# Releasing K's weights at the start: a gate of two elements in place of a gate behind a large write

## The chip, the cores and the metric

The kernel runs on one core of one Trainium2 chip. The metric is the device time of one execution in microseconds (us), the median over several executions. Each execution also gives the span of the core (first to last instruction, some 1.7 us shorter than the time) and the mean granted clock of TensorE. A profile is one execution; its times count from the start of the span.

## The reference, cut to what matters

```python
x  = A_x                                   # 2048 x 576
xn = layernorm(x)
q, k, v = split_heads(xn @ wqkv)           # 32 heads of 18
pq, pk  = phi(q), phi(k)                   # phi(t) = t + 1 or exp(t), plus 1e-6
o   = linear_attention(pq, pk, v)
out = x + o @ wo + (gelu(xn @ w_gate) * (xn @ w_up)) @ w_down
```

The first 14 us of the kernel: the first tiles of x (128 rows each) are loaded, normalised and transposed, K's 576 x 576 weights are loaded, and the first products xn @ K are made.

## The kernel before: the parts that the argument touches

The loads. SP issues x; ScalarE issues K's weights (`which == 1`) once, at the start; Q's weights and the next tiles of x are let go later, by another two-element write.

```python
def load_x(n0, cnt):
    nc.sync.dma_start(x_sb[:, n0:n0 + cnt, :], x_view[:, n0:n0 + cnt, :])

def load_w(which, on=nc.sync):
    c = slice(which * D, (which + 1) * D)
    on.dma_start(wqkv_sb[:, 0:4, c], A_wqkv[0:512, c].rearrange("(kt p) c -> p kt c", p=P))
    on.dma_start(wqkv_sb[0:HP, 4, c], A_wqkv[512:576, c])
    ...
nc.scalar.preload_act_table_set("natural_log_exp_and_others")
load_x(0, 1)
load_x(1, 1)
load_x(2, 2)

nc.vector.memset(wqkv_sb[HP:P, 4, :], 0.0)          # L119: zero padding, 64 x 1728
nc.vector.memset(wqkv_sb[0:1, 0, D:D + 2], 0.0)     # L120: two elements inside K's target
load_w(1, nc.scalar)                                # so K's load waits for L120
...
spin(NWARM)                                         # 38 filler matmuls: TensorE busy from 1.43 to 5.22 us
```

The second write is a gate. It touches two elements that K's load overwrites, so the load has to wait for it; and because VectorE works in order, it also waits for the large write ahead of it.

## Time and profile before

The time before was 523.56 us (three executions, 523.36 to 523.85). What matters of its trace:

| event | us |
|---|---|
| K's first load issued by ScalarE / landed | 1.95 / 7.37 |
| x tile 1 issued / landed | 1.26 / 3.51 |
| x tiles 2 and 3 issued / landed | 1.73 / 5.64 |
| first transpose of tile 0 on TensorE | 5.48 |
| first K product | 7.41 |
| second half of tile 2's K product (from here on TensorE is the bound) | 12.04 |

The list of loads in the first 20 us, with size and time from issue to landing in the last column:

```profile
wqkv_sb<-in_A_wqkv_dram ACTq DMA_DIRECT2D x1, 576.0 KB, 5.4
...
x_sb<-in_A_x_dram SPq DMA_DIRECT2D x2, 144.0 KB, 2.3
x_sb<-in_A_x_dram SPq DMA_DIRECT2D x1, 288.0 KB, 3.9
```

Line by line: K; x tiles 0 and 1; x tiles 2 and 3.

### The profile page before, as it was taken

How to read it: one execution, taken by the hardware profiler on the slowest of the kernel's cores; microseconds unless marked ns; L12 is line 12 of the kernel's file. 1: busy time of each engine (PE TensorE's matmuls, PEld its weight loads, DVE VectorE, ACT ScalarE, POOL GpSimd, SP SyncE). 2: the span in 40 equal slices, each digit the busy share in tenths (PEclk: the TensorE clock that was granted, in tenths of full speed). 3: DMA queues.
4: the chain of work that ended last, by engine and by line, in shares of the span. 5: the costliest groups of instructions: out<-in, count | busy, mean ns of one | idle time of the engine just before them, and what ended most of it. 6: DMA issues, size and time to landing. Idle time of an engine off the chain costs nothing.

```text
span 521.7 us, 10641 instructions
## 1 busy us (share of the span) xinstructions
PE 516.1 (99%) x4498; PEld 313.5 (60%) x4498; DVE 250.9 (48%) x436; ACT 143.1 (27%) x293; POOL 35.2 (7%) x55
## 2 busy tenths in 40 slices
PE   7999999999999999999999999999999999999997
PEld 6777755555587754444577744444777544445775
DVE  7996565876358323433388133333584233433101
ACT  6898442332320013323200032232000123322000
POOL 2021000211001100000012000000011000000000
PEclk9999999999999999999999999999999999999999
DMA  8334609899500045555300155555100355440000
GB/s 279 62 64 118 154 25 264 254 269 266 157 12 13 13 124 155 144 156 160 93 13 13 41 166 145 155 156 155 29 23 13 103 161 158 140 134 2 13 11 24
DMA packets 106282, 57.89 MB, mean 111 GB/s; under 512 B 13370, under 2 KB 105722, under 8 KB 106234
## 3 DMA queue, kind: packets, MB, share of 16 engines
q1 hardware_dynamic: 105626, 56.55, 38.8%
q8 instruction: 35, 0.57, 0.5%
q10 hardware_dynamic: 608, 0.66, 0.4%
q14 instruction: 13, 0.11, 0.1%
HBM read 52.86 MB, written 2.36 MB: 106 GB/s over the span
## 4 chain that ended last, share of the span: by engine, by line
PE 97%; DMA 1%; ACT 1%; DVE 0%; issue 0%
PE ps_all L313 55%; PE ps_all L677 27%; PE ps_all L289 4%; PE ps_all L682 4%; PE ps_all L245 3%; PE ps_all L342 3%; DMA wqkv_sb<-in_A_wqkv_dram 1%; PE ps_all L451 1%; PE ps_all L433 0%; PE ps_all L659 0%; ACT xnT L234 0%; ACT L114 0%; ACT phi_e L265 0%; ACT phi_e L269 0%; DVE hT L273 0%; DVE res L685 0%
## 5 line engine op out<-in xcount | busy, mean ns | idle before, releaser
L313 PE MATMUL ps_all<-xnT,wg 64*128 64x512 bf16 x1152 | 272.6, 376 | 0.0
L313 PE MATMUL ps_all<-xnT,wu 64*128 64x512 bf16 x1152 | 271.8, 376 | 0.0
L648 DVE TENSOR_TENSOR hT<-ps_all,gl 128x512 bf16<-128x512 f32 x144 | 99.5, 691 | 161.9 <-ACT gl L647 161.2
L647 ACT ACTIVATE gl<-ps_all 128x512 f32<-128x512 f32 x144 | 86.1, 598 | 314.3 <-PE ps_all L313 297.4
L313 PEld LDWEIGHTS <-wu 64*128 64x128 bf16 x1152 | 108.3, 94 | 66.3
L313 PEld LDWEIGHTS <-wg 64*128 64x128 bf16 x1152 | 108.3, 94 | 66.1
L677 PE MATMUL ps_all<-wd_sb,hT 128*128 128x288 bf16 x1152 | 147.0, 286 | 0.0
L677 PEld LDWEIGHTS <-hT 128*128 128x128 bf16 x1152 | 112.3, 98 | 30.6 <-issue 1.3
L475 DVE RECIPROCAL den_sb<-den_sb 126x128 f32<-126x128 f32 (+1 forms) x80 | 68.3, 911 | 0.5
L685 DVE TENSOR_TENSOR res<-ps_all,x_sb 128x288 bf16<-128x288 f32 x32 | 14.7, 458 | 88.0 <-PE ps_all L682 88.0
L313 PE MATMUL ps_all<-xnT,wr 64*128 64x512 bf16 x288 | 55.1, 376 | 0.0
L478 POOL TENSOR_TENSOR pqT<-pqT,den_sb 126x512 bf16<-126x512 bf16 (+3 forms) x25 | 24.2, 966 | 317.3 <-DVE den_sb L475 279.4
L682 PE MATMUL ps_all<-m_sb,pqT 126*128 126x288 bf16 (+1 forms) x160 | 24.9, 285 | 0.0
L313 PEld LDWEIGHTS <-wr 64*128 64x128 bf16 x288 | 14.4, 94 | 16.9 <-issue 0.7
L245 PE MATMUL ps_all<-wqkv_sb,xnT 128*128 128x288 bf16 x160 | 22.5, 286 | 0.9 <-DMA wqkv_sb<-in_A_wqkv_dram 0.8
L289 PE MATMUL ps_all<-hT,xn 128*128 128x288 bf16 (+4 forms) x176 | 22.4, 275 | 0.0
L289 PEld LDWEIGHTS <-xn 128*128 128x128 bf16 (+1 forms) x176 | 17.5, 102 | 4.1
L245 PEld LDWEIGHTS <-xnT 128*128 128x128 bf16 x160 | 15.4, 98 | 6.9 <-issue 1.4
L682 PEld LDWEIGHTS <-pqT 126*128 126x128 bf16 (+1 forms) x160 | 15.5, 97 | 4.1
L342 PE MATMUL ps_all<-xnT,wqkv_sb 128*126 128x512 bf16 (+1 forms) x70 | 17.4, 378 | 0.0
L273 DVE SCALAR_TENSOR_TENSOR hT<-ps_all,phi_e 128x288 bf16<-128x288 f32 x32 | 13.2, 450 | 4.6 <-ACT phi_e L269 4.0
L265 ACT ACTIVATE phi_e<-ps_all 128x288 f32<-128x288 f32 x32 | 12.9, 410 | 3.6 <-PE ps_all L245 2.1
(68 smaller groups left out, 173.8 us busy)
## 6 DMA issues: line engine op xcount, KB each, us to landing
wg<-in_B_w_gate_dram SPq DMA_DIRECT2D x72, 256.0 KB, 2.9
wu<-in_B_w_up_dram SPq DMA_DIRECT2D x72, 256.0 KB, 3.5
wd_sb<-in_B_w_down_dram SPq DMA_DIRECT2D x12, 432.0 KB, 4.6
wr<-in_B_w_gate_dram SPq DMA_DIRECT2D x72, 32.0 KB, 2.7
wr<-in_B_w_up_dram SPq DMA_DIRECT2D x72, 32.0 KB, 3.1
out_dram<-res SPq DMA_DIRECT2D x15, 144.0 KB, 1.8
x_sb<-in_A_x_dram SPq DMA_DIRECT2D x3, 576.0 KB, 7.1
wqkv_sb<-in_A_wqkv_dram SPq DMA_DIRECT2D x2, 576.0 KB, 4.7
```

The costliest lines, as they stand in the source:

```text
L245: nc.tensor.matmul(ps_all[:, k_bank(n, hf), :HALF], lhsT=xnT[:, kt, n * P:(n + 1) * P], rhs=wqkv_sb[:, kt, D + hf * HALF:D + (hf + 1) * HALF],
L273: nc.vector.scalar_tensor_tensor(out=out_, in0=ps, scalar=0.0, in1=e, op0=ALU.max, op1=ALU.add)
L289: nc.tensor.matmul(ps_all[:m, b, col:col + w], lhsT=xn[:, n, j0:j0 + m], rhs=pk[:, n, d0:d0 + w], start=(n == 0 and col == 0), stop=(n == ...
L313: return nc.tensor.matmul(self.outs[i], lhsT=self.lhs(i, rows, kt), rhs=self.rhs(i, rows, kt), start=start, stop=stop, skip_group_check=True,)
L342: nc.tensor.matmul(ps, lhsT=wqkv_sb[:, kt, q0:q0 + rows], rhs=xnT[:, kt, sc * SC:(sc + 1) * SC], start=(kt == 0), stop=(kt == KT - 1),)
L475: nc.vector.reciprocal(out=d[:, h:h + P], in_=d[:, h:h + P])
L478: nc.gpsimd.tensor_tensor(out=pqT[:rows, c, cols], in0=pqT[:rows, c, cols], in1=d, op=ALU.mult)
L647: nc.scalar.activation(out=gl[:], in_=ps_all[:, b[0], :], func=ACT.Gelu_apprx_tanh)
L648: nc.vector.tensor_tensor(out=hT[:, GUB * k + i, :], in0=ps_all[:, b[1], :], in1=gl[:], op=ALU.mult)
L677: nc.tensor.matmul(acc, lhsT=hT[:, f, j * P:(j + 1) * P], rhs=wd_sb[:, f, hs], start=(f == 0), stop=False,)
L682: nc.tensor.matmul(acc, lhsT=pqT[:rows, c, ts_], rhs=m_sb[:rows, c, hs], start=False, stop=(c == NCH - 1),)
L685: nc.vector.tensor_tensor(out=res[:, hs], in0=acc, in1=x_sb[:, n, hs], op=ALU.add)
```

## The change

The intent is to let K's weights go as soon as the program starts, behind the two-element write alone, because TensorE waits 0.8 us for them. It is one moved line:

```diff
-    nc.vector.memset(wqkv_sb[HP:P, 4, :], 0.0)
     nc.vector.memset(wqkv_sb[0:1, 0, D:D + 2], 0.0)
     load_w(1, nc.scalar)
+    nc.vector.memset(wqkv_sb[HP:P, 4, :], 0.0)
```

## The prediction

> **What bounds the kernel now.** I read the whole page first. TensorE is busy 516.1 of 521.7 us, so nothing that leaves TensorE's path as it is can move the time, and what can be won is TensorE's idle time. The view of TensorE's waits names all of it that is worth naming:
>
> ```profile
> PE ps_all L133 <- POOL ident masks.py:199: 1.4, 1, 1.4
> PE ps_all L245 <- DMA wqkv_sb<-in_A_wqkv_dram: 0.8, 1, 0.8
> PE ps_all L231 <- DVE xn L216: 0.3, 1, 0.3
> ```
>
> The reader is to see that in the whole run only one wait of TensorE belongs to the weights this change touches: one wait, 0.8 us. Then the table of windows says where it lies and that nothing after it is loose:
>
> ```profile
> 0.00:7.41 7.41, 4.86 (x52) 4.40 (x52) 5.59 (x21) 3.25 (x8) 2.99 (x16) 1.00 0.76 227
> 7.41:12.04 4.63, 4.49 (x42) 3.39 (x42) 3.34 (x11) 3.76 (x11) 0.59 (x3) 1.00 1.04 339
> 12.04:66.00 53.96, 53.96 (x415) 40.87 (x416) 41.11 (x115) 42.17 (x113) 7.44 (x12) 1.00 0.45 103
> 66.00:515.00 449.00, 449.00 (x3965) 262.07 (x3962) 200.43 (x291) 93.92 (x161) 24.15 (x25) 1.00 0.38 109
> ```
>
> Second column: the length; third: TensorE busy. From 12.04 to 515 us TensorE is busy all the time, so a start that is earlier by some tenths should reach the end whole. Third, the chain of waits over the first 16 us:
>
> ```profile
> 0.80 1.15 ACT L114
> 1.95 5.42 DMA wqkv_sb<-in_A_wqkv_dram
> 7.37 0.04 issue
> 7.41 0.79 PE ps_all L245 x5
> 8.20 0.02 issue
> 8.22 0.41 ACT phi_e L265
> ```
>
> K's weights leave at 1.95, land at 7.37, and the first K product starts 0.04 us later. The chain puts the table load ahead of the transfer, but that is only the instruction before it on ScalarE. The timeline shows what really held it:
>
> ```profile
> 0.80 1.28 ACT L114 ACT_TABLE_LOAD   x1 [0.80 <-PEq L725]
> 1.05 0.78 DVE L119 MEMSET wqkv_sb<- 64x864 uint32 x1 [1.05 <-PEq L725]
> 1.86 0.06 DVE L120 MEMSET wqkv_sb<- 1x1 uint32 x1
> 1.95 0.44 ACTq L109 DMA_DIRECT2D wqkv_sb<-in_A_wqkv_dram  x1
> ```
>
> The table load runs until 2.08, the transfer is issued at 1.95: it does not wait for the load. It comes 0.03 us after the end of the two-element write (1.86 + 0.06 = 1.92), and that write stands behind the large one on VectorE.
>
> **What the Trainium skill says.** (1) "DMA: Bandwidth & Descriptors", section "Anatomy of one DMA": DMA engines do not wait on semaphores; a wait is made on the issuing sequencer, before dispatch. The trace agrees: 1.92 to 1.95. (2) Same page, "Issuing engines are not separate DMA queues": "DMAs initiated by the scalar, sync or gpsimd engine will ultimately run on the same 16 DMA engines and interleave with each other". That is the main caution: an earlier K shares with x. The trace agrees that the engines are full: x's queue q1 and K's queue q10 together keep about 98% of the 16 engines from 2.0 to 5.6 us. (3) Same page, "Queues, rings and completion order": each DMA engine goes round between its queues packet by packet, so K will not wait until x is done once its descriptors are there. In the window 3.8 to 5.6 both queues do move (lines below). (4) "VectorE: DVE Perf Modes", section "Zero memsets can be issued as uint32": a memset takes a cycle per element. The trace has 64x864 at 778 ns, 0.90 ns per element along a row, and 59 ns for one element.
>
> **The change part by part.** It moves one line; it removes and adds none. The built programs differ only in the order of these two writes on VectorE; TensorE, ScalarE, GpSimd and SP keep their instructions, and the transfer now waits for the first VectorE signal instead of the second. The large write touches other partitions (64 to 127 of the fifth slab) than the transfers, so it gets no wait on them.
> - VectorE: the same two writes, 0.78 + 0.06 us, in the other order. Its next real work is the first x tile's statistics at 3.14, with 0.48 us idle before. Cost: 0.
> - The issue: the small write starts at 1.05, ends at 1.11, plus 0.03 gives 1.14. K's first transfer leaves 1.95 - 1.14 = 0.81 us earlier, the second (72 KB) 1.61 instead of 2.42.
> - The first packet: before, q10 moves nothing until 3.8, though K left at 1.95:
>
> ```profile
> q1 hardware_dynamic: 350, 0.46, 98.4%
> ...
> q10 hardware_dynamic: 426, 0.49, 81.7%
> q1 hardware_dynamic: 64, 0.11, 17.5%
> ...
> q1 hardware_dynamic: 93, 0.43, 79.0%
> q10 hardware_dynamic: 182, 0.18, 30.0%
> ```
>
> (Three windows: 2.0 to 3.8, 3.8 to 5.6 and 5.6 to 7.4 us; packets, MB, share of the engines.) If the 1.9 us from issue to first packet are its own, K's packets start at about 3.1. V's weights, the same shape, later show 1.25 us from issue (47.17) to first packet (48.4) on an idle queue; with that K would start at 2.4. I take 2.4 to 3.1.
> - The landing: the engines are full from 2.0 us on, so bytes are not made, only reordered. The first four tiles of x (0.59 MB) and K (0.66 MB) are 1.25 MB. But from 5.6 on K's last packets share with the next x load, of 4608-byte packets, and with 0.81 us more in front K has fewer packets left by then. Landing moves from 7.37 by less than 0.81: I take 0.4 to 0.8, so 6.6 to 7.0.
> - TensorE: the K product also needs the first tile's transposes, copied by VectorE at 6.65 to 6.89, and TensorE's filler ends at 6.62. So the start cannot come forward by more than 0.79 us.
> - The price: x tiles 2 and 3 leave at about 1.73 and land 3.9 us later, at 5.63; VectorE wants them at 5.67. There is no slack. If K pushes them to 5.9 or 6.0, the statistics there start 0.3 later, and with them, in VectorE's order, the copy for the first K product (to 6.95 to 7.19) and tile 1's normalisation. The last two of its five matmuls then start at 7.2 instead of about 7.75: about 0.5 of the 0.79 stays, and behind tile 1's transposes 0.3 to 0.4.
> - Passing on: from 8.22 to 11.5 the chain runs on ScalarE, nearly full, so an earlier first relu moves it whole; at 12.04 TensorE takes over. Later inputs have slack: x tile 4 lands at about 9.0 for 10.35, Q's weights at about 11.8 for 13.48.
>
> Sum: 0.79 at most, less 0.3 to 0.5 of delayed x: about 0.4 us. 523.56 - 0.36 = 523.2.
>
> **The rivals.** (a) Nothing lost: x keeps its times, K lands by 6.7, 0.75 us won, 522.8. For it: x's packets of 3.0 to 3.8 are alone in their queue and the bytes per us are low there (255 GB/s over the window against 332 after), so K may fill unused time. Against it: the engines count as 98% busy. (b) K takes the place of x: issued at 1.14 it is now ahead of x tile 1 (about 1.26) and tiles 2 and 3 (1.73), not behind them. If descriptors are made in order of issue, for 512 rows of K against 128 of a tile, x lands up to 1 us later, VectorE falls behind, and the wait of TensorE moves from the DMA to the copy: 0 won, or 0.3 lost, 523.6 to 523.9. For it: q10's silence until 3.8, as if K had stood in line behind x. (c) The transfer is hidden anyway: against it stands the direct release at 7.37 to 7.41. I give the main line 50%, (a) 20%, (b) 30%.
>
> **Range and chances.** Every rival lies within 0.8 us, 0.15%, of 523.56, and three runs before spread over 0.5 us. So faster or slower by over 2% (10.5 us) would need an altogether different state of the chip. The range is 522.5 to 523.9: the full win with some spread, to rival (b) with some.
>
> **What would show it.** K's issue on ScalarE's queue at about 1.14 proves the release; a first q10 packet at 2.4 to 3.1 the start; tiles 2 and 3 landing over 4.1 us after issue the price; the first L245 at 6.8 to 7.2, with its DMA wait under 0.5 us, the gain. TensorE's start of the K product, halves 0 and 1, must then be early by a like amount at 12.04. If x's statistics wait on a DMA for over 0.5 us, (b) holds. The prediction is wrong if the issue does not move (a wait on ScalarE that I do not see) or if x is starved by more than 1 us.

## More of the kernel before

The order in which each engine's instructions are written is set by a table of numbers. They sort the program text; they are no times of the chip.

```python
STEPS = [
    (ln_stats, [3.15, 4.09, 5.57, ...]),             # VectorE, tile 0, 1, 2, ...
    (ln_rstd,  [4.27, 5.21, 6.69, ...]),             # ScalarE
    (ln_norm,  [x_, 6.78, 8.06, ...]),               # VectorE; tile 0 at 5.03 and 5.41
    ...
]
todo += [(4.0, lambda n: nc.vector.memset(x_sb[0:1, n, 0:2], 0.0), 4)]
todo += [(4.01, lambda n: load_x(n, 4), n) for n in (4,)]
todo += [(4.02, lambda n: load_w(0), 0)] + [(4.03, lambda n: load_x(n, 4), n) for n in (8, 12)]
```

So VectorE takes the statistics of tiles 0 and 1, then tile 0's normalisation, then the statistics of tiles 2 and 3 and on.

## The result, and the profile after

The changed kernel took 525.40 us (median of four, 524.75 to 525.66), the one before 523.68 in the same rounds. The ratio is 1.0032, with a 95% interval of 1.0014 to 1.0049. Ratios here are the mean time of one kernel's fast executions over that of the other's in the same rounds, so they are not quite the ratio of the medians. By its interval it is slower, by about 1.7 us, where 0.4 us of gain had been predicted.

K did come early. The chain of waits of the changed kernel's first 30 us no longer has it:

```profile
1.26 4.57 DMA x_sb<-in_A_x_dram
5.83 0.02 issue
5.85 0.83 DVE stats L207 x2
6.68 0.02 issue
6.71 0.21 DVE mv L208
6.91 0.49 DVE xn L216 x2
```

In K's place stands x tile 1: issued at 1.26 as before, landed at 5.83 in place of 3.51. The list of loads says the same:

```profile
wqkv_sb<-in_A_wqkv_dram ACTq DMA_DIRECT2D x1, 576.0 KB, 4.6
...
x_sb<-in_A_x_dram SPq DMA_DIRECT2D x2, 144.0 KB, 3.6
x_sb<-in_A_x_dram SPq DMA_DIRECT2D x1, 288.0 KB, 5.0
```

The 3.6 is the median of two unlike loads (2.6 for tile 0, 4.6 for tile 1): a median of a group hides that one member went wrong. K, issued at 0.95, landed at 5.55. What the queues moved shows how. These are the window from 3.2 to 4.0 us after, then the same window before (packets, MB, share of the engines; q1 is SP's queue and carries x, q10 is ScalarE's and carries K):

```profile
q10 hardware_dynamic: 267, 0.31, 106.5%
```

```profile
q1 hardware_dynamic: 80, 0.17, 76.0%
q10 hardware_dynamic: 11, 0.01, 5.6%
```

After, not one packet of x moves in these 0.8 us, though tile 1 had been issued 1.9 us before the window begins. This is not sharing packet by packet; tile 1 stands behind K.

VectorE's timeline shows what the late tile holds up:

```profile
0.86 0.06 DVE L119 MEMSET wqkv_sb<- 1x1 uint32 x1 [0.86 <-PEq L725]
...
5.85 0.82 DVE L207 BATCH_NORM_STATS2 stats<-x_sb 128x6 f32<-128x288 bf16 x2 [1.31 <-DMA x_sb<-in_A_x_dram]
6.71 0.21 DVE L208 BATCH_NORM_AGGREGATE mv<-stats 128x2 f32<-128x12 f32 x1
6.83 0.57 DVE L216 TENSOR_SCALAR xn<-x_sb,mv,rstd 128x384 bf16<-128x384 bf16 x2
```

The bracket is idle time and what ended it. Tile 0 is on the core at 3.45, but its normalisation (6.83; 5.10 before) stands in VectorE's order behind tile 1's statistics. TensorE's wait for K, 0.8 us, is gone, and another has come:

```profile
PE ps_all L231 <- DVE xn L216: 2.0, 1, 2.0
```

That is tile 0's transpose, waiting for the normalised tile. And then the clock falls. The windows view for 8.0 to 11.4 us, before and after, where the first column after the window is its length, the next TensorE busy with its number of matmuls, and the third number from the end is the granted clock:

```profile
8.00:11.40 3.40, 3.32 (x33) 2.49 (x31) 2.27 (x7) 3.15 (x10) 0.48 (x2) 1.00 1.06 326
```

```profile
8.00:11.40 3.40, 3.40 (x23) 2.52 (x22) 2.08 (x9) 2.07 (x7) 0.47 (x2) 0.50 1.07 363
```

TensorE is "busy" all the time in both, but at half clock it did 23 matmuls in place of 33. The page would not show this by its busy shares: a throttled engine looks fuller. In numbers at TensorE: first transpose +1.73 us, first K product +0.92 (it had been 0.8 late for K before), second half of tile 2's K product +1.82. Every later point keeps this; the gate and up projections begin at 67.51 in place of 65.71.

### The profile page after: what moved, and what is told of

Its sections match the earlier page's. It is cut to its first block, busy times and chain, and to the rows that moved or that the text cites. A ratio compares the mean times of both kernels' runs of the same rounds, so it can differ in the third digit from the quotient of the medians.

```text
span 523.5 us, 10641 instructions
## 1 busy us (share of the span) xinstructions
PE 517.1 (99%) x4498; PEld 314.5 (60%) x4498; DVE 250.9 (48%) x436; ACT 143.2 (27%) x293; POOL 35.2 (7%) x55
## 4 chain that ended last, share of the span: by engine, by line
PE 98%; DMA 1%; DVE 0%; SPq 0%; issue 0%; POOL 0%; POOLq 0%
PE ps_all L313 55%; PE ps_all L677 27%; PE ps_all L245 4%; PE ps_all L289 4%; PE ps_all L682 4%; PE ps_all L342 3%; DMA x_sb<-in_A_x_dram 1%; PE ps_all L451 1%; PE ps_all L433 0%; PE ps_all L659 0%; PE ps_all L231 0%; DVE stats L207 0%; PE ps_all L133 0%; DVE xn L216 0%; DVE res L685 0%; SPq L93 0%
## 5 line engine op out<-in xcount | busy, mean ns | idle before, releaser
L245 PE MATMUL ps_all<-wqkv_sb,xnT 128*128 128x288 bf16 x160 | 23.6, 296 | 0.0
L207 DVE BATCH_NORM_STATS2 stats<-x_sb 128x6 f32<-128x288 bf16 x32 | 13.0, 448 | 2.0 <-DMA x_sb<-in_A_x_dram 2.0
```

Of the source, the lines that this page charges most:

```text
L245: nc.tensor.matmul(ps_all[:, k_bank(n, hf), :HALF], lhsT=xnT[:, kt, n * P:(n + 1) * P], rhs=wqkv_sb[:, kt, D + hf * HALF:D + (hf + 1) * HALF],
```

## The experiments

Twelve runs. The theory: **loads are handed out in one line, in about the order of their issue, whichever queue they are on**; K now stands ahead of x tiles 1 to 3, tile 1 comes 2.3 us late, and TensorE's idle gap costs it the clock on top. Rivals: the two queues share packet by packet and only K's bytes matter; VectorE's in-order work is the real loss; the clock is the whole loss. The table collects what the sections below use; "tile 2" is the start of the second half of tile 2's K product (12.04 before).

| run | K issued / landed | x tile 1 landed | x tiles 2, 3 landed | first K product | tile 2 | time, ratio [95%] |
|---|---|---|---|---|---|---|
| before | 1.95 / 7.37 | 3.51 | 5.64 | 7.41 | 12.04 | 523.6 |
| after | 0.95 / 5.55 | 5.83 | 6.73 | 8.33 | 13.86 | 525.40, 1.0032 [1.0014, 1.0049] |
| a_again | 0.95 / 5.73 | 6.00 | 6.92 | 8.36 | 13.17 | 526.05, 1.0038 [1.0026, 1.0050] |
| e1_warm | 0.95 / 5.37 | 5.68 | 6.65 | 8.04 | 12.85 | 525.13, 1.0027 [1.0015, 1.0039] |
| e2_tile0_first | 0.95 / 5.50 | 5.91 | 6.85 | 6.83 | 13.29 | 524.77, 1.0020 [1.0007, 1.0033] |
| e3_between | 1.50 / 8.14 | 3.63 | 7.13 | 8.18 | 12.86 | 524.91, 1.0025 [1.0009, 1.0041] |
| e4_behind | 1.77 / 7.27 | 3.63 | 5.49 | 7.31 | 11.94 | 523.54, 0.9995 [0.9980, 1.0009] |
| e5_slabs | 0.95 / 6.93 | 4.21 | 6.53 | 6.76 | 12.26 | 524.35, 1.0008 [0.9990, 1.0026] |
| e6_one_queue | 1.26 / 5.65 | 6.25 | 7.00 | 9.00 | 14.46 | 525.85, one look |
| e7_next_x_later | 1.95 / 6.91 | 3.48 | 4.72 | 6.95 | 11.76 | 523.42, 0.9993 [0.9978, 1.0007] |
| e8_second | 1.07 / 5.86 | 5.06 | 6.86 | 7.42 | 12.58 | 524.78, 1.0014 [0.9999, 1.0028] |
| e9_behind_later | 1.77 / 6.90 | 3.50 | 5.40 | 6.94 | 11.58 | 523.27, 0.9986 [0.9974, 0.9999] |
| e10_second_order | 1.07 / 6.27 | 5.83 | 7.09 | 8.63 | 14.22 | 524.97, 1.0019 [1.0005, 1.0032] |
| e9_again | 1.77 / 7.01 | 3.63 | 5.42 | 7.05 | 11.68 | 523.15, 0.9986 [0.9970, 1.0002] |

(K landed means its 512-row load; in e5_slabs, the last slab of it.)

Two cautions for the table. First, the trace records the arrival of each of these loads in 16 parts, and "landed" is the last of the 16. Where most parts are in time and one or two are late, the text below says so. Second, the mean granted clock counts only what the clock record holds. A mean of 1.000 does not prove a full clock: in e6 the record begins at 10.73 us and in e10 there is none, both are listed with 1.000, and in both TensorE's matmuls near 9 us start 0.24 us apart in place of 0.12. So the counts of executions with a fallen clock below are counts of falls that the record shows, and may be too low.

### a_again: the changed kernel once more

No edit.

> The changed kernel once more, beside the others. Both theories: 525.0 to 525.7 us, x tile 1 landing near 5.8 us. It also shows whether the halved clock of TensorE (8.0 to 11.4 us in the first trace) comes back in another execution.

The six executions fall in two groups. Two, of 524.5 and 524.6 us, have a granted clock of 1.000; four, of 525.95 to 526.39, have 0.996 or 0.997. The profiled one is of the first group, and in its window TensorE does 34 matmuls at full clock:

```profile
8.00:11.40 3.40, 3.33 (x34) 2.43 (x35) 2.91 (x10) 2.86 (x10) 0.47 (x2) 1.00 1.07 368
```

Its x tile 1 is as late (6.00), yet tile 2's product is at 13.17, not 13.86. So by these two traces the late tile alone costs about 1.1 us of TensorE's time, and the half clock, where it strikes, another 0.7. The two sets of the changed kernel together: five executions at full clock with a mean span of 523.28, five with the fall with 524.28. The kernel before, beside all the experiments, had the fall in 4 of 40 executions (mean span 523.48, against 521.98 for the 36 others). I had expected 525.0 to 525.7; the median, 526.05, is above that and the spread is wider. By the second caution above, some executions counted as of full clock may not be: two of the changed kernel's with 1.000 took 525.55 and 525.66 us, longer than its profiled one with the fall (525.26).

### e1_warm: TensorE kept busy over the gap

```diff
-NWARM = 38
+NWARM = 74
```

> The changed kernel with 74 warm-up matmuls in place of 38, so that TensorE stays busy over its 2.0 us wait for the first transposes. If the halved clock from 8.0 to 11.4 us is a cost of its own, it is gone here (clock 1.00 in that window) and the time falls by 0.7 to 1.2 us, to 524.2 to 524.8. If the late x tile alone sets the time, it stays at 525.2 to 525.7.

No fall of the clock is recorded in any of the five executions, and the profiled one has 35 matmuls at 1.00 in the window. Tile 2's product came to 12.85, 1.0 us ahead of the changed kernel's first trace. The time fell only to 525.13, above the range I gave. The trace shows where the rest went: TensorE loses another 0.5 us near 45 us, at a wait on a DMA transpose of a later tile (0.3 of it visible as a wait). A packet of instructions (16 KB, queue q8) runs on one of the DMA engines in those microseconds, and the filler matmuls shift when it comes. e2 has a like stall. That the packet causes it is argued, not tested; the kernel before has such a packet too, at 45.09, and no stall. So the clock is a part of the loss and not the whole: with a full clock the changed kernel is still slower by 1.0027.

### e2_tile0_first: tile 0 not behind tile 1 on VectorE

```diff
-        (ln_stats, [3.15, 4.09, 5.57, ...]),
-        (ln_rstd, [4.27, 5.21, 6.69, ...]),
+        (ln_stats, [3.15, 6.52, 6.53, ...]),
+        (ln_rstd, [4.27, 6.54, 6.69, ...]),
```

> The changed kernel with VectorE's order changed: tile 0's normalisation and copy stand before the statistics of tiles 1 and 2. If what hurts is VectorE waiting in order for x tile 1, tile 0's transposes start near 5.3 to 5.6 us instead of 7.2, the first K product near 6.3 to 6.8 instead of 8.3, and the time falls to 523.8 to 524.8. If tile 1's own landing near 5.8 us sets the pace behind it anyway, the time stays at 525.0 to 525.5 although the first K product is early.

The first K product came at 6.83, 0.6 us ahead of the kernel before. It did not help, as TensorE's line for the next tile shows:

```profile
6.83 0.79 PE L245 MATMUL ps_all<-wqkv_sb,xnT 128*128 128x288 bf16 x5
9.21 0.53 PE L231 MATMUL ps_all<-ident,xn 128*128 128x128 bf16 x5 [1.59 <-DVE xn L216]
```

Tile 1's transposes start at 9.21 (8.02 before): TensorE's wait has moved one tile on. Tile 2's product is at 13.29, no earlier than in a_again (13.17). So in these traces VectorE's order decides where TensorE waits, not how late tile 2's product is; tile 1's landing sets the pace. That rival falls by the trace, not by the time: 524.77 us lies in the range of my first branch (523.8 to 524.8), which was to speak for the rival. The median is better than a_again's, and none of the five executions has a recorded fall of the clock. That this is because the gap now stands later, behind work, was not tested.

### e3_between, e4_behind, e8_second: where K stands in the line

The gate is a part of the large write, so that its length sets K's issue:

```diff
-    nc.vector.memset(wqkv_sb[0:1, 0, D:D + 2], 0.0)
+    nc.vector.memset(wqkv_sb[HP:P, 4, 0:C], 0.0); nc.vector.memset(wqkv_sb[0:1, 0, D:D + 2], 0.0)
     load_w(1, nc.scalar)
-    nc.vector.memset(wqkv_sb[HP:P, 4, :], 0.0)
+    nc.vector.memset(wqkv_sb[HP:P, 4, C:3 * D], 0.0)
```

with C = 860 (e3), 1380 (e4) and 40 (e8).

> The gate ahead of K is a part of the large write, so that K leaves at about 1.4 us: behind x tile 1 (1.26) and ahead of x tiles 2 and 3 (1.73). If loads are served in order of issue over both queues, x tile 1 lands at 3.5 to 3.9 us as in the kernel before, x tiles 2 and 3 land at 6.0 to 6.9, K at 5.6 to 6.2, and the time is 523.4 to 524.3. If the queues share the engines packet by packet from the start, x tile 1 is late too, at 4.3 us or more, in proportion to K's earlier start.

> The gate ahead of K is most of the large write: K leaves at about 1.75 to 1.85 us, 0.1 to 0.2 earlier than in the kernel before but still behind the issue of x tiles 2 and 3 (1.73). If the place in the line of loads is what counts, x tiles 1 to 3 keep their landings (3.5 and 5.2 to 5.9 us), K lands at 7.0 to 7.4, and the time is 523.3 to 523.8, as before. If every tenth of earlier issue delays x in proportion, tiles 2 and 3 land past 6.0 and the time is 523.8 to 524.5.

> The gate ahead of K is a very short write, so that K leaves at about 1.2 us, 0.06 ahead of x tile 1 (1.26). If a load takes its place in the line when its issue starts, K is still ahead: x tile 1 lands at 5.4 to 6.0 us and the time is that of the changed kernel, 524.5 to 526.2. If the place is taken a quarter of a microsecond later for K (the run with K at 1.50 looked like that), x tile 1 is ahead and lands at 3.4 to 4.0, x tiles 2 and 3 stand behind all of K and land at 5.9 to 6.9, K lands at 5.6 to 6.6, and VectorE waits about 0.5 to 1.2 us for tiles 2 and 3: 523.8 to 524.6 us.

e4: K issued 0.04 us after tiles 2 and 3 lets them land at 5.49, as before, and no packet of K moves until 3.7 us, though it was issued at 1.77. The time is that of the kernel before, as the theory said.

e3: K issued after tile 1 leaves tile 1 alone (3.63), and tiles 2 and 3, issued 0.23 us after K, land at 7.13 in place of 5.64. So the order of issue decides which of x's loads suffers. Not all of the delay is the order's, though: the eighth of the 16 parts of tiles 2 and 3 came at 5.42 (4.41 before), the fifteenth at 5.90, and one late part at 7.13. The time, 524.91, is above the range I gave, and three of its six executions had the fallen clock. Two things in the trace were not as expected. K itself landed later than before, at 8.14, and TensorE waited 1.2 us for it; here too 15 of the 16 parts were there by 7.20, and one was 0.9 us behind. Why one part lags is open. And from 3.8 to 5.0 us both queues moved:

```profile
q1 hardware_dynamic: 113, 0.25, 54.5%
q10 hardware_dynamic: 135, 0.16, 39.5%
```

113 packets of x against 135 of K: nearly turn by turn. A strict line would have held x back until K was out.

e8: K issued 0.19 us ahead of tile 1 gives the case between: tile 1 lands at 5.06, neither 3.5 nor 5.8, and 524.78 us. Neither of my two branches fits: the first has the time but not the landing, the second neither. In e10, below, the same gate gave 5.83, but there 15 of tile 1's 16 parts had come by 5.19, and only the last was late; the changed kernel's first part came at 5.14. So in these traces, with K 0.31 us ahead of a load of x the latter stands behind most of K, with 0.19 and 0.23 the two share, and with K 0.04 behind x, K waits. What fixes a load's place within those 0.3 us stays open.

### e5_slabs: K in four loads

```diff
-        on.dma_start(wqkv_sb[:, 0:4, c], A_wqkv[0:512, c].rearrange(...))
+        for k0, k1 in ([(0, 1), (1, 2), (2, 3), (3, 4)] if which == 1 else [(0, 4)]):
+            on.dma_start(wqkv_sb[:, k0:k1, c], A_wqkv[k0 * P:k1 * P, c].rearrange(...))
```

> The changed kernel with K's 512 rows cut into four loads of 128 rows on ScalarE's queue, issued about every 0.45 us from 0.95 on, so that x's loads fall between them. If a load holds up all that are issued after it, on either queue, until its own rows are handed out, x tile 1 now waits for 128 rows of K in place of 512 and lands at 3.8 to 4.5 us in place of 5.8, tiles 2 and 3 at 4.9 to 5.9, K's last slab at 6.3 to 7.2, and the time is 523.0 to 524.0. If what delays x is only that K's bytes move earlier, x tile 1 stays past 5.0 us and the time stays at 524.5 or more.

This is the test that tells the line from the sharing of bytes: the same rows of K, with the same gate, but x may step between them. Tile 1 landed at 4.21 in place of 5.8. K's third slab was issued at 1.85, 0.12 us after x tiles 2 and 3, and in the window 4.0 to 4.4 us it is the one that stands:

```profile
q1 hardware_dynamic: 59, 0.14, 87.4%
q10 hardware_dynamic: 9, 0.01, 4.5%
```

So the line works in both directions, and neither queue has right of way. Most of the loss is gone (tile 2's product at 12.26, +0.2 us). It does not beat the kernel before: tiles 2 and 3 land at 6.53, past the range I gave, and VectorE waits 0.6 us for them. Of their 16 parts 14 had come by 5.36 and the last two at 6.52 and 6.53, so the late landing is that of two parts. The time, 524.35, is above that range too, and its interval does not tell it from no change.

### e6_one_queue: the same order on one queue

```diff
     load_x(0, 1)
+    nc.vector.memset(wqkv_sb[0:1, 0, D:D + 2], 0.0)
+    load_w(1, nc.sync)
     load_x(1, 1)
     load_x(2, 2)
-    nc.vector.memset(wqkv_sb[0:1, 0, D:D + 2], 0.0)
-    load_w(1, nc.scalar)
```

> The changed kernel with K issued from SP, between x tiles 0 and 1, so that all loads are on one queue in the order that the changed kernel gives them. If two queues are served as one line in order of issue, x tile 1 lands at 5.5 to 6.3 us as in the changed kernel (5.8). If ScalarE's queue is served ahead of SP's and that is what starves x, x tile 1 is late here only by SP's own issue time (about 0.5 us each for the two loads of K) and its landing is at 4.5 to 5.2.

Tile 1 lands at 6.25, in the first branch's range; SP's own issues put it at 2.33 in place of 1.26. I must qualify the run: within one queue tile 1 stands behind K anyway, so it cannot by itself rule out a right of way of ScalarE's queue. By the landings (6.25 against 5.83 and 6.00) the second queue won the changed kernel little over plain in-order loading. Its time and its later columns say less: K's matmuls at 9.0 us start 0.24 us apart and the clock record begins only at 10.73, so this execution had a half clock too, although the listed mean is 1.000. e4 and e5, where K waits behind x, rule the right of way out.

### e7_next_x_later: what K's last rows share with

In the kernel before, the loads of x tiles 4 to 7 and of Q's weights are let go one step later:

```diff
-todo += [(4.0, lambda n: nc.vector.memset(x_sb[0:1, n, 0:2], 0.0), 4)]
+todo += [(4.10, lambda n: nc.vector.memset(x_sb[0:1, n, 0:2], 0.0), 4)]
```

and likewise 4.01 to 4.03 become 4.11 to 4.13, so that they stand behind tile 1's statistics (4.09).

> The kernel before, with the loads of x tiles 4 to 7 and of Q's weights let go after tile 1's statistics in place of tile 0's: issue at about 5.1 in place of 4.25 us, so that K's last rows share the engines with nothing. If K's landing at 7.37 is held up by those loads from 5.6 us on, it comes to 6.6 to 7.0 and the time falls by 0.2 to 0.6, to 523.0 to 523.4. If K's slowest engine is late for another reason, nothing changes; if the later loads then miss their own time (first transposed tile needed at about 17.0 us, landing 16.2 before), the time rises.

They are issued at 5.10 in place of 4.25; K lands at 6.91 in place of 7.37, the first K product starts at 6.95, and tile 2's product is 0.28 us earlier. The time, 523.42 against 523.63, points the same way, but the interval includes no change. Tiles 2 and 3 also landed earlier, at 4.72 in place of 5.64; whether the step did that is not shown, as e9, with the same step and K at 1.77, has 5.40 and 5.42.

### e9_behind_later and e9_again: both small steps

The gate of e4 and the later loads of e7.

> Two small changes together: K issued at about 1.77 us, just behind x tiles 2 and 3, and the loads of x tiles 4 to 7 and Q's weights let go after tile 1's statistics. In the traces each of them alone moved TensorE's work after 12 us forward, by 0.1 and 0.28 us. If they add, 523.2 us or less, 0.3 to 0.4 below the kernel before beside it; if the first K product is by then held by the first tile's copy (ready at about 6.9 us) and not by K, it stays at what the later loads alone gave, 0.1 to 0.3 below.

> The version with K at about 1.77 us and the later loads let go after tile 1's statistics, once more, because its first interval (0.9974 to 0.9999) only just excludes no change. If the gain is real, the ratio is 0.998 to 0.9995 again, K lands near 6.9 us and the first K product starts near 6.95 (7.41 before). If the first time was luck with the executions of before, the ratio is 1.000.

K lands at 6.90 and 7.01, the wait for it is gone, and tile 2's product is at 11.58 and 11.68, 0.46 and 0.36 us ahead of the kernel before. TensorE's waits in e9_behind_later are the first matmul's and nothing else over the listing's threshold:

```profile
PE ps_all L133 <- POOL ident masks.py:199: 1.4, 1, 1.4
```

Both times the ratio is 0.9986: 523.27 against 523.88 and 523.15 against 523.63. The medians are 0.6 and 0.5 us below the kernel before, and about 2 us below the changed one. The first interval just excludes no change, the second, up to 1.0002, just includes it. Some of the gain is not the steps' own: three of the 20 executions of before in those two comparisons had the fallen clock, and none of the 11 of this version has one on record. The traces, at full clock, give 0.4 us.

### e10_second_order: K early and VectorE reordered

e8's gate, e7's later loads, and tile 2's statistics moved behind tile 1's normalisation (5.57 becomes 6.79, tile 2's rstd 6.69 becomes 6.80).

> As the run with K at 1.2 us, with the later loads let go after tile 1's statistics, and with VectorE's statistics of tile 2 moved behind tile 0's copy and tile 1's normalisation, so that nothing that K's first products need stands behind the late tiles 2 and 3. If K is behind x tile 1 in the line, the first K product starts at 6.3 to 6.8 us (7.41 before), tile 1's transposes at 7.2 to 7.6, and the time is 522.9 to 523.5. If K is ahead of x tile 1, tile 0's chain stands behind tile 1's statistics at 5.8 and the time is 524.5 to 526.

K was ahead of tile 1 (landed at 5.83), and the time is 524.97, in the range of that branch. This order on VectorE did not repair a late tile 1, but the run is no clean test of that, for two reasons. Here the later loads were a mistake of mine: they hang on tile 1's statistics, so they were let go at 6.96. In its profile the first K matmuls start 0.24 us apart, as in the changed kernel's slow stretch, against 0.12 in the kernel before, so the clock was halved in this execution too, although the windows view gives 1.00: this trace has no clock record at all.

## Why the prediction was wrong, point by point

- **The bound, and what passes on: right.** A shift at tile 2's K product reached the end: +1.82 us there, +1.80 at 67.5 us.
- **The release: right in kind, wrong in size.** It said issue at 1.14; it was 0.95, because VectorE started the small write at 0.86, not at the 1.05 of the large one. K's first packet came at 2.37, at the early end of the 2.4 to 3.1 given. Whether 1.14 would have hurt less stays open: with K at 1.07 tile 1 landed at 5.06 in e8 and at 5.83 in e10 (15 of its 16 parts by 5.19), late in both.
- **TensorE's DMA wait for K: right that it goes.** It went, and K landed at 5.55, a microsecond earlier than the 6.6 to 7.0 predicted, because it ran alone (no packet of x from 3.2 to 4.0).
- **The step that failed**: "each DMA engine goes round between its queues packet by packet, so K will not wait until x is done once its descriptors are there". The sentence is about packets that are there. Tile 1's, it seems, were not: none of it moved from 3.2 to 4.0 us, though it was issued at 1.26. (The trace shows packets, not how descriptors are made; e4 and e5 show that the order of issue decides.) The sum therefore took "less 0.3 to 0.5 of delayed x", for tiles 2 and 3 alone, and left tile 1 out. Measured: tiles 2 and 3 1.1 us late, tile 1 2.3 us late, 1.1 us of it at TensorE (a_again). Rival (b) had named the mechanism, "if descriptors are made in order of issue", and had read the silence of K's queue until 3.8 us as its sign; it was the right theory, at 30%, and too small: it put x up to 1 us late, where tile 1 was 2.3, and 0.3 us lost at most, where 1.7 were.
- **The term that was missing: the clock.** The 2.0 us gap was followed by half clock for 3.4 us in the first trace; in 5 of 10 executions the recorded mean clock shows such a fall. "TensorE: Matmul & The Clock Gate", section "What's actually happening", has what was needed: the clock follows the activity in a free-running window of 3413 ns. The trace agrees: its clock record is full from 4.60, half from 8.01 and full again from 11.42 us, two stretches of 3.41. In the one before the fall TensorE was busy for 1.35 us. The free phase fits that another execution of the same program escapes: in a_again the record begins at 5.67, so the gap lies otherwise in the windows, and in the one from 5.67 to 9.08 TensorE was busy for 1.64 us. Mean spans with and without the fall differ by 1.0 us in the changed kernel. In e1 no fall is on record in five executions of five.
- **The range** of 522.5 to 523.9 covered every rival as I had sized it, and so failed with them: 525.40. That nothing would move by 2% came true.

## What to carry to other kernels

A gate on a load is also a place in a line. Before letting a large load go earlier, list every load that is issued after its new place, with its landing and the moment it is wanted; a small one that was just in time (here tile 1, wanted at 4.1 us, landed at 3.5) can come to wait for most of the large one, and in these runs another queue did not let it pass. Here, cutting the large load into pieces took most of the loss away but won nothing over the kernel before (e5); moving it only up to its neighbour and clearing what competes with its end gave some 0.4 us in the traces (e9). And a gap of TensorE early in a kernel can cost more than its length, because the clock may fall after it.

## What the Trainium skill lacked or had wrong

- "DMA: Bandwidth & Descriptors", sections "Queues, rings and completion order" and "Issuing engines are not separate DMA queues": they give the turn-taking of the DMA engines and say that loads "interleave with each other". They do not say for this chip that a load may hand out no rows until an earlier-issued load of the other queue is nearly out. Here: tile 1 issued at 1.26, no packet from 3.2 to 4.0 us while 267 packets of K moved; in the kernel before and in e4 it is K that stands, until 3.88 and 3.7 us. With issues 0.23 us apart both moved (113 and 135 packets in 1.2 us, e3).
- "TensorE: Matmul & The Clock Gate", section "Why this matters for your kernels": it advises no idle gap over about 3 us. Here a gap of 2.0 us was followed by half clock in at least 5 of 10 executions, and the kernel before, with gaps of 0.8 us and less in its trace, fell in at least 4 of 40. The window before the fall was not idle: TensorE was busy for 1.35 of its 3.41 us.
- The same page's caution, section "Seeing it yourself", that clock records can be unreliable was met: one trace (e10_second_order) has none, and its matmuls, 0.24 us apart in place of 0.12, show the half clock all the same. In e6 the record begins at 10.73, so the mean of 1.000 leaves out the slow start.
